# Moving the last block's routing between engines and reordering the first expert tiles in a fused attention and two-mixture kernel

## The chip, the cores and the metric

The kernel runs on one core of a Trainium2 chip. The metric is device time in microseconds (us) from launch to end, taken as the median of several executions; one further execution is profiled, and its trace is what all rows below come from. Engines are named as the profile names them: PE (matmul; PEld is its weight load), DVE (vector), ACT (scalar), POOL (GpSimd) and SP (the queue that issues most DMA transfers). Each engine works through its own instructions strictly in program order and waits on semaphores for the others.

## The reference

Three stages, 1152 rows (tokens) of 512 columns between them. The change lies where the third begins.

```python
x = attention(q, k, v, f)                 # 2 batches x 8 heads x 576 x 64, causal, with decay from f
x = moe(x, domain_probs, w1, w2)          # dense: all 4 experts on every row

def moe2(x, w_skip, w_gate, w1, w2):      # routed: 8 experts, one for each row
    do_compute = x @ w_skip > 0           # the other rows are returned as they are
    xc = x[do_compute]
    logits = xc @ w_gate
    e_idx = argmax(logits, axis=1)
    probs = softmax(logits)
    gate_w = probs[row, e_idx]
    y[e_idx == e] = gate_w * (relu(xc[e_idx == e] @ w1[e]) @ w2[e])
    out[do_compute] = xc + y
```

## The kernel before

Rows are worked in nine blocks of 128 (NB = 9, so L = 8 is the last). The dense mixture ends with its last half expert's down products: `down_block` (36 matmuls a block on PE), then `add_block` on DVE, which leaves the block's final rows in `acc[:, t]`. While PE still works on later blocks, each finished block is routed by a plan written out by hand (`plan`, `planned`): `store` writes it to the output and, for the first five blocks, to a DRAM copy `xda`; `turn` transposes it; `logits` (or the folded form) gives nine columns, eight gate scores and the skip score; `choose` (five small DVE instructions) makes the one-hot mask `mall` of the chosen expert; `prefix` counts with two small matmuls how many earlier rows chose the same expert and puts that rank into `rank`; `slots` turns the rank into a one-hot row of 128 slots (`onehot`); `keep` stores `d` (scores less their maximum) and two token numbers into `perm`; `count` adds the mask to a running sum `macc`; `tokens` multiplies `onehot` by `perm`, which gives for each expert the list of its rows in slot order (`pids`).

Two blocks, 7 and 8, are still to be routed when the last down product is done, and nothing of the dense stage is left to lie beside them. This stretch, from the end of `down_block` for block 8 (line 989 on) to the first expert's up products, I call the turn. The order there is the order of the code: the scheduler is in manual mode, and each engine takes its instructions as written.

The routed stage works with small tiles. For each expert e the first 64 rows in its list are half rows of 256 columns on 128 partitions (two partitions a row), handled by class `Few`: `x_in` transposes them on PE and copies them with ACT into `xt`, `up(0)` and `up(1)` multiply by the up weights (eight matmuls in all, seen as sixteen passes in the trace, since each f32 matmul shows as two), a relu on ACT gives `hs`, `turn` transposes that on PE and copies it in two halves (DVE, then ACT) into `ht`, and `down` multiplies by the down weights (sixteen matmuls, 32 passes), after which DVE adds the gated result to the rows (`xes[e]`) and POOL scatters them to the output. Experts with over 64 rows spill into two further tiles of class `Many`. The rows of experts 1 to 7 come by an indirect DMA issued on POOL (`gather`), from lists that `idx` holds. Expert 0 is not gathered, so that PE has work at once: its rows of blocks 0 to 4 come early from `xda` into `xs0`; its rows of blocks 5 to 8 are picked out of `acc` on chip, by `mine` (the mask's first column as f32), `pick` (a 128x64 one-hot matrix `sel`) and `select` (matmuls of `sel` with `acc`, summed over the blocks in the PSUM bank `xsel`). `xs0` plus `xsel` is then transposed and copied into `xt0`.

Weights of the routed stage come in chunks of 1 MB into a ring of 17 places, in the order of use; `load_m` issues them on SP, and each waits until its place is free. Chunks 0 to 14 are issued before or in the turn. Chunks 15 and 16 go to a pool (`wraw2`) that takes over memory of the routing pools, so they wait for the last routing work that uses it, which is `weigh` (softmax weights for blocks 3 to 8: exponentials on ACT, then DVE). Chunks 17 and 18 take the places of expert 0's up weights, 19 and 20 those of its down weights, 21 and 22 those of expert 1's up weights. `heat` is two matmuls whose result nobody reads.

After the turn, before the change, PE does: up of tile 0; `gates` (nine small matmuls on `perm`, which wait for `weigh`); turn of tile 0; x_in of tile 1; down of tile 0; up(0) of tile 1; x_in of tile 2; up(1) of tile 1; then a loop whose step i does up(0) of tile i+1, turn of tile i, x_in of tile i+2, up(1) of tile i+1, down of tile i. `place` and `spread` on DVE prepare the lists for the two spill tiles.

Of the kernel before, what the change touches and what calls it, by code (L numbers as in the profile page):

```python
# [7 lines left out]
F32 = mybir.dt.float32  # L8
# [39 lines left out]
def kernel(  # L48
# [613 lines left out]
    with ExitStack() as mo:  # L662
# [19 lines left out]
                T.transpose(ps[:, (c - c0) * P:(c - c0 + 1) * P], acc[:, t, c * P:(c + 1) * P], ident)  # L682
            A.copy(out=xt[:, c0 * P:c1 * P], in_=ps[:, 0:(c1 - c0) * P])

        def logits(t, lp):
            xt = rt[t]["xt"]
            rt[t]["lp"] = lp
            for c in range(KD):
                T.matmul(out=lp[:, 0:E2 + 1], lhsT=xt[:, c * P:(c + 1) * P], rhs=wgs[:, c, :],
                         start=(c == 0), stop=(c == KD - 1))  # L690

# [191 lines left out]
        def cleared(t):  # L883
            rows = hida_p.tile([P, 8, HD], F32, tag="hh0", name="rows")
            rowo = hida_p.tile([P, 8, HD], F32, tag="hl0", name="rowo")
            G.memset(rows[:, 1:E2], 0.0)
            G.memset(rowo[:, 0:2 * KO], 0.0)
            xes.extend([xs0] + [rows[:, e] for e in range(1, E2)])
            xos.extend(rowo[:, 2 * k:2 * k + 2].rearrange("p a c -> p (a c)") for k in range(KO))
            ys.extend(rowo[:, 2 * KO + i] for i in range(4))  # L890

# [96 lines left out]
        def heat(n):  # L988
            for _ in range(n):
                T.matmul(out=hot[:, 0:3 * P], lhsT=ones, rhs=onehot[:, 0:3, :], start=True, stop=True)  # L990

        L = NB - 1
        for tb in range(NA - 1, NB):
            ps = down_block(UL, tb, planned)
            if tb < L:
                add_block(UL, tb, ps, 0, DM)
        h = DM // 2
        logits(L - 1, ps_r.tile([P, 512], F32, tag="lg", name=f"lg_{L - 1}"))
        add_block(UL, L, ps, 0, h)
# [5 lines left out]
        store(L)  # L1005
        load_m(13, 15)
        pf = ps_d.tile([P, 512], F32, tag="d", name="pf")
        hot = ps_d.tile([P, 512], F32, tag="d", name="hot")
        xsel = ps_u.tile([P, 512], F32, tag="u", name="xsel")

        def mine(t):
            m32 = rt[t]["m32"] = rtile([P, 1], "m32", t)
            V.tensor_copy(out=m32, in_=mall[:, t, 0:1])

        def pick(t):
            m32 = rt[t]["m32"]
            V.tensor_scalar(out=sel[:, t - NX, :], in0=slotn[:, 0:RT], scalar1=rank[:, t:t + 1],
                            scalar2=m32, op0=ALU.is_equal, op1=ALU.mult)

        def select(t):  # L1020
            for g in range(2):
                T.matmul(out=xsel[RT * g:RT * g + RT, 0:HD], lhsT=sel[:, t - NX, :],
                         rhs=acc[:, t, g * HD:(g + 1) * HD], start=(t == NX), stop=(t == L))

        for t in range(NX, NA):
            mine(t)
            pick(t)
        choose(L - 1)
        mine(L - 1)
        count(L - 1)  # L1030
        select(NX)
        logits(L, ps_u.tile([P, 512], F32, tag="u", name=f"lg_{L}"))
        keep(L - 1)
        prefix(L - 1, pf)
        for t in range(NX + 1, NA):
            select(t)
        heat(2)
        choose(L)
        mine(L)
        pick(L - 1)  # L1040
        pf = ps_u.tile([P, 512], F32, tag="u", name="pf_L")
        prefix(L, pf)
        select(L - 1)
        pick(L)
        select(L)
        slots(L - 1)
        V.tensor_tensor(out=xs0, in0=xsel[:, 0:HD], in1=xs0, op=ALU.add)
        heat(2)
        slots(L)
        keep(L)  # L1050
        count(L)
        xtp0 = ps_r.tile([P, 512], F32, tag="xp", name="xtp0")
        for c in range(2):
            T.transpose(xtp0[:, c * P:(c + 1) * P], xs0[:, c * P:(c + 1) * P], ident)
        A.copy(out=xt0, in_=xtp0[:, 0:HD])
        tokens(L - 1)
        tokens(L)
        V.scalar_tensor_tensor(out=idx, in0=pids[:, 1, :], scalar=2.0, in1=pida, op0=ALU.mult, op1=ALU.add)
        T.matmul(out=pf[:, E2:2 * E2], lhsT=ones, rhs=macc[L], start=True, stop=True)
        V.tensor_copy(out=cnt, in_=pf[:, E2:2 * E2])  # L1060
        weigh(3, NB)

# [55 lines left out]
    class Few:  # L1118
# [12 lines left out]
        def up(self, half):  # L1131
            for c in range(2 * half, 2 * half + 2):
                g, j = divmod(c, 2)
                for h in range(2):
                    T.matmul(out=self.ps[RT * h:RT * h + RT, :], lhsT=self.xt[:, j * P + RT * g:j * P + RT * g + RT],
                             rhs=wm[0, self.e, h][:, c, :], start=(c == 0), stop=(c == KD - 1))
            if half:
                A.activation(out=self.hs[:, 0:HF], in_=self.ps, func=AF.Relu)

        def turn(self):  # L1140
            for j in range(4):
# [132 lines left out]
        listed(po, KO, idxo, gato)  # L1274

    tiles = [Few(e) for e in range(E2)] + [Many(k) for k in range(KO)]
    for e in range(1, E2):
        gather(xes[e], idx[:, e:e + 1])
    load_m(15, NS + 2)
    tiles[0].up(0)  # L1280
    tiles[0].up(1)
    gates()
    tiles[0].turn()
    tiles[1].x_in()
    tiles[0].down()
    place()
    tiles[1].up(0)
    tiles[2].x_in()
    tiles[1].up(1)
    spread(0, NB)  # L1290
    ahead = {(E2 - 3, 1): [(0, 0, 0)], (E2 - 2, 1): [(0, 0, 1)], (E2 - 1, 0): [(1, 0, 0)],
             (E2 - 1, 1): [(1, 0, 1), (0, 1, 0)], (E2, 0): [(0, 1, 1)], (E2, 1): [(1, 1, 0), (1, 1, 1)]}

# [120 lines left out]
```

## Time and profile before

| | us |
|---|---|
| median of 3 executions | 605.55 |
| lowest, highest | 604.0, 605.95 |
| the profiled execution's own time | 604.57 |
| span of its trace, first to last instruction | 602.9 |

| engine | busy us | share of the span |
|---|---|---|
| PE | 588.6 | 98% |
| PEld | 489.5 | 81% |
| POOL | 331.1 | 55% |
| DVE | 321.8 | 53% |
| ACT | 262.2 | 44% |

The profiled execution's time is 1.67 us longer than its span, and 0.98 us under the median. A share is a mean over stages: PE's 98% says that PE is the engine to follow, and only the stretches where it is not at work without a break, or works on what nobody needs, can give time back. The times of rows are us from the span's start.

### The profile page before, as it was taken

The numbers are of one execution on the slowest core, as the hardware profiler recorded it, in microseconds if no ns is written. First come the engines' busy times: TensorE is split into PE (matmuls) and PEld (weight loads), VectorE is DVE, ScalarE is ACT, GpSimd is POOL, SyncE is SP. The second block draws the span as 40 slices with busy tenths as digits, with TensorE's granted clock in tenths as the row PEclk, the third lists the DMA queues.
The fourth block names the chain that finished last, engine by engine and source line by source line (L and its number), as shares of the span: only waits on it lengthen the run. The fifth ranks groups of instructions, "written<-read, shape, count | busy, mean of one in ns | idle before, by whom it ended". The sixth has DMA issues, their size and how long they took to land. (4 is left out here: it accounts for less than half of the span.)

```text
span 602.9 us, 10704 instructions
## 1 busy us (share of the span) xinstructions
PE 588.6 (98%) x3975; PEld 489.5 (81%) x3975; DVE 321.8 (53%) x826; ACT 262.2 (44%) x665; POOL 331.1 (55%) x380
## 2 busy tenths in 40 slices
PE   8999899999999999999999999999999999999995
PEld 5788777998898998998988989989989774555674
DVE  6877877655444544534535535535535466411483
ACT  5678788684243343334324315315314222112481
POOL 4869997799268159249339429519615143222421
PEclk7899999999999999999999999999999999999998
DMA  6786550301111011101202201202255975999940
GB/s 209 229 308 212 186 187 23 132 16 67 70 70 62 10 52 35 55 8 63 71 1 70 72 1 70 71 1 70 71 210 212 369 276 194 416 418 421 401 157 24
DMA packets 19127, 84.22 MB, mean 140 GB/s; under 512 B 2943, under 2 KB 3977, under 8 KB 11905
## 3 DMA queue, kind: packets, MB, share of 16 engines
q1 hardware_dynamic: 16832, 73.19, 33.3%
q0 software_dynamic: 2240, 10.32, 4.4%
q8 instruction: 32, 0.52, 0.4%
q14 instruction: 23, 0.18, 0.1%
HBM read 79.44 MB, written 5.28 MB: 141 GB/s over the span
## 5 line engine op out<-in xcount | busy, mean ns | idle before, releaser
L865 PE MATMUL dn<-w2h,hh 128*128 128x512 f32 x288 | 114.4, 397 | 0.0
L867 PE MATMUL dn<-w2h,hl 128*128 128x512 f32 x288 | 112.5, 391 | 0.0
L866 PE MATMUL dn<-w2l,hh 128*128 128x512 f32 x288 | 112.2, 390 | 0.0
L877 DVE SCALAR_TENSOR_TENSOR acc<-dn,dps,acc 128x512 f32<-128x512 f32 (+1 forms) x64 | 47.4, 742 | 98.3 <-PE dn L867 98.2
L156 POOL TENSOR_TENSOR w2l<-rawd,w2h 128x512 fp32r<-128x512 f32 x32 | 40.5, 1296 | 94.4 <-ACT w2h L201 94.4
L220 PE MATMUL p<-xb_h,w 128*128 128x320 f32 x224 | 69.2, 309 | 0.0
L219 PE MATMUL p<-xb_l,w 128*128 128x320 f32 x224 | 69.2, 309 | 0.0
L218 PE MATMUL p<-xb_h,w 128*128 128x320 f32 x224 | 69.1, 309 | 0.0
L867 PEld LDWEIGHTS dn<-w2h,hl 128*128 128x128 f32 x288 | 54.0, 188 | 11.6
L865 PEld LDWEIGHTS dn<-w2h,hh 128*128 128x128 f32 x288 | 54.1, 188 | 11.2 <-issue 1.4
L866 PEld LDWEIGHTS dn<-w2l,hh 128*128 128x128 f32 x288 | 54.1, 188 | 10.0
L218 PE MATMUL p<-xa,w 128*128 128x256 f32 x218 | 61.3, 281 | 0.0
L220 PE MATMUL p<-xa,w 128*128 128x256 f32 x218 | 61.2, 281 | 0.0
L219 PE MATMUL p<-xa,w 128*128 128x256 f32 x218 | 61.2, 281 | 0.0
L201 ACT CAST w2h<-rawd 128x512 fp32r<-128x512 f32 x32 | 18.3, 622 | 84.7 <-PE dn L867 84.7
L156 POOL TENSOR_TENSOR hl<-m,hh 128x256 fp32r<-128x256 f32 (+1 forms) x32 | 25.9, 810 | 43.5 <-ACT hh L827 43.5
L821 DVE SCALAR_TENSOR_TENSOR hl<-p,hh 128x320 fp32r<-128x320 f32 (+1 forms) x62 | 28.5, 459 | 36.1 <-ACT hh L820 36.1
L156 POOL TENSOR_TENSOR w<-ws,w 128x512 fp32r<-128x512 f32 x32 | 40.7, 1294 | 3.4 <-ACT w L175 3.4
L219 PEld LDWEIGHTS p<-xb_l,w 128*128 128x128 f32 x224 | 42.0, 188 | 0.3
L218 PEld LDWEIGHTS p<-xb_h,w 128*128 128x128 f32 x224 | 42.1, 188 | 0.3
L220 PEld LDWEIGHTS p<-xb_h,w 128*128 128x128 f32 x224 | 42.0, 188 | 0.0
L218 PEld LDWEIGHTS p<-xa,w 128*128 128x128 f32 x218 | 41.3, 190 | 0.3
(292 smaller groups left out, 1329.0 us busy)
## 6 DMA issues: line engine op xcount, KB each, us to landing
wm<-in_m SPq DMA_DIRECT2D x32, 1024.0 KB, 9.7
rawu<-in_w SPq DMA_DIRECT2D x8, 1024.0 KB, 4.7
rawd<-in_w SPq DMA_DIRECT2D x8, 1024.0 KB, 4.7
qk<-in_qk SPq DMA_DIRECT2D x7, 640.0 KB, 5.5
qk<-in_qk SPq DMA_DIRECT2D x7, 576.0 KB, 4.0
bias<-nbd SPq DMA_DIRECT2D x14, 288.0 KB, 6.1
v<-in_v SPq DMA_DIRECT2D x8, 320.0 KB, 3.0
bias<-nbd SPq DMA_DIRECT2D x16, 144.0 KB, 5.9
```

The source lines that it names most:

```text
L156: eng.tensor_tensor(out=out, in0=a, in1=b, op=ALU.subtract)
L201: A.copy(out=ws["d", u][0][:, c, :], in_=wr["d", u][:, c, :])
L218: T.matmul(out=ps, lhsT=wt[:, 0, a, i, :], rhs=xh[:, i, :], start=(i == 0), stop=False)
L219: T.matmul(out=ps, lhsT=wt[:, 0, a, i, :], rhs=xl[:, i, :], start=False, stop=False)
L220: T.matmul(out=ps, lhsT=wt[:, 1, a, i, :], rhs=xh[:, i, :], start=False, stop=(i == 1))
L821: V.scalar_tensor_tensor(out=hl[:, j, cs], in0=c, scalar=0.0, in1=hh[:, j, cs].bitcast(F32), op0=ALU.max, op1=ALU.subtract)
L865: T.matmul(out=ps, lhsT=hh[:, j, ks], rhs=wh[:, j, :], start=(j == 0), stop=False)
L866: T.matmul(out=ps, lhsT=hh[:, j, ks], rhs=wl[:, j, :], start=False, stop=False)
L867: T.matmul(out=ps, lhsT=hl[:, j, ks], rhs=wh[:, j, :], start=False, stop=(j == 3))
L877: V.scalar_tensor_tensor(out=a, in0=ps[:, c0:c1], scalar=pe, in1=a, op0=ALU.mult, op1=ALU.add)
```

## The change

In the turn, `mine`, `pick` for blocks 5 and 6, `count` and the token part of `keep` go from DVE to POOL; `pick` for blocks 7 and 8 stays on DVE. `logits` of block 8 is split in two, with the prefix of block 7 between. Block 8's rows of expert 0 are no longer selected into `xsel`: the sum of blocks 5 to 7 is added to `xs0` earlier, transposed by matmuls with `ident` into a new bank `xtl`, and four more matmuls with `acc` as the weights and `sel` as the moving operand add block 8's rows into the same open bank, already transposed. `xt0` is copied out of it in two halves, by ACT and by DVE. The second `heat` moves behind the count of all rows.

Since `xs0` now lacks block 8's rows, the rows that tile 0's result is added to come by an eighth gather, second in the order (1, 0, 2 to 7); `rows` is cleared whole. In the first body x_in and up(0) of tile 1 stand directly behind tile 0's up products, its turn, `gates` and `spread` behind those, and its down products behind up(1) of tile 1.

```diff
--- before.py
+++ after.py
@@ -682,10 +682,10 @@
                 T.transpose(ps[:, (c - c0) * P:(c - c0 + 1) * P], acc[:, t, c * P:(c + 1) * P], ident)
             A.copy(out=xt[:, c0 * P:c1 * P], in_=ps[:, 0:(c1 - c0) * P])
 
-        def logits(t, lp):
+        def logits(t, lp, c0=0, c1=KD):
             xt = rt[t]["xt"]
             rt[t]["lp"] = lp
-            for c in range(KD):
+            for c in range(c0, c1):
                 T.matmul(out=lp[:, 0:E2 + 1], lhsT=xt[:, c * P:(c + 1) * P], rhs=wgs[:, c, :],
                          start=(c == 0), stop=(c == KD - 1))
 
@@ -883,9 +883,9 @@
         def cleared(t):
             rows = hida_p.tile([P, 8, HD], F32, tag="hh0", name="rows")
             rowo = hida_p.tile([P, 8, HD], F32, tag="hl0", name="rowo")
-            G.memset(rows[:, 1:E2], 0.0)
+            G.memset(rows, 0.0)
             G.memset(rowo[:, 0:2 * KO], 0.0)
-            xes.extend([xs0] + [rows[:, e] for e in range(1, E2)])
+            xes.extend(rows[:, e] for e in range(E2))
             xos.extend(rowo[:, 2 * k:2 * k + 2].rearrange("p a c -> p (a c)") for k in range(KO))
             ys.extend(rowo[:, 2 * KO + i] for i in range(4))
 
@@ -989,11 +989,27 @@
             for _ in range(n):
                 T.matmul(out=hot[:, 0:3 * P], lhsT=ones, rhs=onehot[:, 0:3, :], start=True, stop=True)
 
+        def mine(t, eng=V):
+            m32 = rt[t]["m32"] = rtile([P, 1], "m32", t)
+            eng.tensor_copy(out=m32, in_=mall[:, t, 0:1])
+
+        def pick(t, eng=V):
+            eng.tensor_scalar(out=sel[:, t - NX, :], in0=slotn[:, 0:RT], scalar1=rank[:, t:t + 1],
+                              scalar2=rt[t]["m32"], op0=ALU.is_equal, op1=ALU.mult)
+
+        def select(t):
+            for g in range(2):
+                T.matmul(out=xsel[RT * g:RT * g + RT, 0:HD], lhsT=sel[:, t - NX, :],
+                         rhs=acc[:, t, g * HD:(g + 1) * HD], start=(t == NX), stop=(t == L - 1))
+
         L = NB - 1
         for tb in range(NA - 1, NB):
             ps = down_block(UL, tb, planned)
             if tb < L:
                 add_block(UL, tb, ps, 0, DM)
+        for t in range(NX, NA):
+            mine(t, G)
+            pick(t, G)
         h = DM // 2
         logits(L - 1, ps_r.tile([P, 512], F32, tag="lg", name=f"lg_{L - 1}"))
         add_block(UL, L, ps, 0, h)
@@ -1005,58 +1021,45 @@
         store(L)
         load_m(13, 15)
         pf = ps_d.tile([P, 512], F32, tag="d", name="pf")
-        hot = ps_d.tile([P, 512], F32, tag="d", name="hot")
         xsel = ps_u.tile([P, 512], F32, tag="u", name="xsel")
-
-        def mine(t):
-            m32 = rt[t]["m32"] = rtile([P, 1], "m32", t)
-            V.tensor_copy(out=m32, in_=mall[:, t, 0:1])
-
-        def pick(t):
-            m32 = rt[t]["m32"]
-            V.tensor_scalar(out=sel[:, t - NX, :], in0=slotn[:, 0:RT], scalar1=rank[:, t:t + 1],
-                            scalar2=m32, op0=ALU.is_equal, op1=ALU.mult)
-
-        def select(t):
-            for g in range(2):
-                T.matmul(out=xsel[RT * g:RT * g + RT, 0:HD], lhsT=sel[:, t - NX, :],
-                         rhs=acc[:, t, g * HD:(g + 1) * HD], start=(t == NX), stop=(t == L))
-
-        for t in range(NX, NA):
-            mine(t)
-            pick(t)
         choose(L - 1)
-        mine(L - 1)
-        count(L - 1)
+        mine(L - 1, G)
+        count(L - 1, G)
         select(NX)
-        logits(L, ps_u.tile([P, 512], F32, tag="u", name=f"lg_{L}"))
-        keep(L - 1)
+        lgl = ps_u.tile([P, 512], F32, tag="u", name=f"lg_{L}")
+        logits(L, lgl, 0, 2)
         prefix(L - 1, pf)
-        for t in range(NX + 1, NA):
+        pick(L - 1)
+        logits(L, lgl, 2, 4)
+        for t in range(NX + 1, L):
             select(t)
+        keep(L - 1, G)
+        choose(L)
+        mine(L, G)
+        V.tensor_tensor(out=xs0, in0=xsel[:, 0:HD], in1=xs0, op=ALU.add)
+        hot = ps_r.tile([P, 512], F32, tag="xp", name="hot")
+        xtl = ps_d.tile([P, 512], F32, tag="d", name="xtl")
         heat(2)
-        choose(L)
-        mine(L)
-        pick(L - 1)
         pf = ps_u.tile([P, 512], F32, tag="u", name="pf_L")
         prefix(L, pf)
-        select(L - 1)
         pick(L)
-        select(L)
+        for c in range(2):
+            T.matmul(out=xtl[:, c * P:(c + 1) * P], lhsT=xs0[:, c * P:(c + 1) * P], rhs=ident, start=(c == 0), stop=False)
+        for c in range(KD):
+            g, j = divmod(c, 2)
+            T.matmul(out=xtl[:, j * P + RT * g:j * P + RT * g + RT], lhsT=acc[:, L, c * P:(c + 1) * P],
+                     rhs=sel[:, L - NX, :], start=False, stop=(c == KD - 1))
         slots(L - 1)
-        V.tensor_tensor(out=xs0, in0=xsel[:, 0:HD], in1=xs0, op=ALU.add)
-        heat(2)
         slots(L)
-        keep(L)
-        count(L)
-        xtp0 = ps_r.tile([P, 512], F32, tag="xp", name="xtp0")
-        for c in range(2):
-            T.transpose(xtp0[:, c * P:(c + 1) * P], xs0[:, c * P:(c + 1) * P], ident)
-        A.copy(out=xt0, in_=xtp0[:, 0:HD])
+        A.copy(out=xt0[:, 0:P], in_=xtl[:, 0:P])
+        V.tensor_copy(out=xt0[:, P:HD], in_=xtl[:, P:HD])
+        keep(L, G)
+        count(L, G)
         tokens(L - 1)
         tokens(L)
         V.scalar_tensor_tensor(out=idx, in0=pids[:, 1, :], scalar=2.0, in1=pida, op0=ALU.mult, op1=ALU.add)
         T.matmul(out=pf[:, E2:2 * E2], lhsT=ones, rhs=macc[L], start=True, stop=True)
+        heat(2)
         V.tensor_copy(out=cnt, in_=pf[:, E2:2 * E2])
         weigh(3, NB)
 
@@ -1134,8 +1137,11 @@
                 for h in range(2):
                     T.matmul(out=self.ps[RT * h:RT * h + RT, :], lhsT=self.xt[:, j * P + RT * g:j * P + RT * g + RT],
                              rhs=wm[0, self.e, h][:, c, :], start=(c == 0), stop=(c == KD - 1))
-            if half:
-                A.activation(out=self.hs[:, 0:HF], in_=self.ps, func=AF.Relu)
+            if half and self.e:
+                self.relu()
+
+        def relu(self):
+            A.activation(out=self.hs[:, 0:HF], in_=self.ps, func=AF.Relu)
 
         def turn(self):
             for j in range(4):
@@ -1274,20 +1280,21 @@
         listed(po, KO, idxo, gato)
 
     tiles = [Few(e) for e in range(E2)] + [Many(k) for k in range(KO)]
-    for e in range(1, E2):
+    for e in (1, 0, *range(2, E2)):
         gather(xes[e], idx[:, e:e + 1])
     load_m(15, NS + 2)
     tiles[0].up(0)
     tiles[0].up(1)
-    gates()
-    tiles[0].turn()
     tiles[1].x_in()
-    tiles[0].down()
+    tiles[0].relu()
     place()
     tiles[1].up(0)
+    tiles[0].turn()
+    gates()
+    spread(0, NB)
     tiles[2].x_in()
     tiles[1].up(1)
-    spread(0, NB)
+    tiles[0].down()
     ahead = {(E2 - 3, 1): [(0, 0, 0)], (E2 - 2, 1): [(0, 0, 1)], (E2 - 1, 0): [(1, 0, 0)],
              (E2 - 1, 1): [(1, 0, 1), (0, 1, 0)], (E2, 0): [(0, 1, 1)], (E2, 1): [(1, 1, 0), (1, 1, 1)]}
 
```

On DVE, from the last block's additions to the start of block 8's choice. `m` is what `mine` makes, `lg` the scores, `pr` and `rank` the prefix. Before, five rows stand between the mask of block 7 and its prefix, and four more (`m` and `sel` of blocks 5 and 6) stand ahead of the first row here:

```order
L708 TENSOR_REDUCE mx_6121<-lg_6089 128x1
L710 SCALAR_TENSOR_TENSOR sc_6123<-lg_6089,mx_6121,rev 128x8
L712 TENSOR_REDUCE sm_6125<-sc_6123 128x1
L714 TENSOR_SCALAR msk_6127<-lg_6089 128x1
L716 SCALAR_TENSOR_TENSOR mall<-sc_6123,sm_6125,msk_6127 128x8
L1013 CAST m_7_6130<-mall 128x1
L744 TENSOR_TENSOR macc_6132<-macc_6084,mall 128x8
L723 TENSOR_SCALAR d_6141<-lg_6089,mx_6121 128x8
L724 TENSOR_SCALAR perm<-mall,tokp 128x8
L725 TENSOR_SCALAR perm<-mall 128x8
L733 ISA pr_6147,rank<-pf,mall 128x8
```

The same place on DVE now:

```order
L712 TENSOR_REDUCE sm_6124<-sc_6122 128x1
L714 TENSOR_SCALAR msk_6126<-lg_6095 128x1
L716 SCALAR_TENSOR_TENSOR mall<-sc_6122,sm_6124,msk_6126 128x8
L733 ISA pr_6140,rank<-pf,mall 128x8
L733 ISA rank 128x1
L997 TENSOR_SCALAR sel<-slotn,rank,m_7_6129 128x64
L723 TENSOR_SCALAR d_6149<-lg_6095,mx_6120 128x8
L708 TENSOR_REDUCE mx_6153<-lg_6135 128x1
```

The prefix now follows the mask directly, and block 7's `pick` (`sel`) has moved ahead of block 8's choice, where it stood behind it.

On PE, the end of the turn, as the difference; `pf_L` is block 8's prefix, `xtp` the old transposed bank, `xtl` the new one:

```order
-L1022 MATMUL xsel<-acc,sel 64x256 x4
-L990 LDWEIGHTS ones
-L990 MATMUL hot<-onehot,ones 128x384
-L990 LDWEIGHTS ones
-L990 MATMUL hot<-onehot,ones 128x384
-L1054 MATMUL xtp_6186<-ident,xs_2078 128x128 x2
+L731 MATMUL pf_L<-macc_6131,ones 128x8
+L1047 MATMUL xtl<-ident,xs_2078 128x128 x2
+L1050 MATMUL xtl<-sel,acc 128x64 x4
```

Block 8's selection, with its way through DVE and back, is replaced by four products behind the transposes.

On PE, the first body now, from tile 0's last up products (`up` with weights `wm` of chunk 1) to its turn (`tp<-ident,hs`); `tpx<-ident,rows` is x_in of tile 1:

```order
L1138 MATMUL up_6263<-wm_5387,xt_2079 64x512
L1131 MATMUL tpx<-ident,rows 128x128 x2
L1138 MATMUL up_6264<-wm_5617,xt_6241 64x512
L1138 MATMUL up_6264<-wm_5627,xt_6241 64x512
L1138 MATMUL up_6264<-wm_5617,xt_6241 64x512
L1138 MATMUL up_6264<-wm_5627,xt_6241 64x512
L1148 MATMUL tp<-ident,hs_6246 128x128 x4
```

Up(0) of tile 1 needs the copy of what the instruction just ahead of it makes; before, turn of tile 0 and down of tile 0 stood around x_in.

## Rows read from the trace of the kernel before

Timeline rows give start, duration, engine, line, operation, output from inputs, shapes and a count; in brackets stands the idle time just before and what ended it. In the first group the columns are the stretch, its length, then PE, PEld, DVE, ACT and POOL busy time (instructions), granted PE clock, DMA share and GB/s.

**Rows 1.** Busy time by stretch: around the turn, and the expert bodies.

```profile
500.00:510.00 10.00, 9.39 (x62) 4.09 (x61) 7.58 (x47) 2.24 (x16) 2.96 (x3) 1.00 0.74 263
520.00:596.00 76.00, 75.76 (x492) 46.67 (x489) 30.95 (x45) 28.13 (x45) 20.58 (x19) 1.00 0.79 320
```

**Rows 2.** Timeline of DVE in the turn.

```profile
499.04 0.88 DVE L877 SCALAR_TENSOR_TENSOR acc<-dn,dps,acc 128x256 f32<-128x256 f32 x2 [0.28 <-PE dn L867]
...
500.65 0.16 DVE L708 TENSOR_REDUCE mx<-lg 128x1 f32<-128x8 f32 x1
...
502.22 0.16 DVE L708 TENSOR_REDUCE mx<-lg 128x1 f32<-128x8 f32 x1
...
502.94 0.23 DVE L716 SCALAR_TENSOR_TENSOR mall<-sc,sm,msk 128x8 bf16<-128x8 f32 x1
...
503.70 0.31 DVE L1017 TENSOR_SCALAR sel<-slotn,rank,m 128x64 f32<-128x64 f32 x1
...
504.76 0.42 DVE L1047 TENSOR_TENSOR xs<-xsel,xs 128x256 f32<-128x256 f32 x1 [0.56 <-PE xsel L1022]
...
505.98 0.17 DVE L1058 SCALAR_TENSOR_TENSOR idx<-pids,pida 128x8 int32<-128x8 f32 x1 [0.19 <-PE pids L750]
```

**Rows 3.** Timeline of PE and ACT in the turn.

```profile
498.84 0.95 PE L689 MATMUL lg<-wgs,xt 128*128 128x9 f32 x8
...
500.47 0.38 ACT L683 COPY xt<-xpb 128x256 f32<-128x256 f32 x1
...
500.96 1.06 PE L689 MATMUL lg<-wgs,xt 128*128 128x9 f32 x8
...
504.65 0.50 PE L990 MATMUL hot<-onehot,ones 128*128 128x384 bf16 x2
...
505.25 0.44 PE L1054 MATMUL xtp<-ident,xs 128*128 128x128 f32 x2
...
505.72 0.37 ACT L1055 COPY xt<-xtp 128x256 f32<-128x256 f32 x1 [4.87 <-PE pids L750]
...
506.15 3.65 PE L1135 MATMUL up<-wm,xt 128*64 128x512 f32 x16
```

**Rows 4.** Timeline of PE in the first bodies.

```profile
510.19 0.30 PE L1228 MATMUL yp<-perm,onehot 128*128 128x24 bf16 x6 [0.22 <-DVE perm L770]
...
511.76 3.67 PE L1150 MATMUL yp<-wm,ht 128*64 128x256 f32 x32 [0.30 <-DVE ht L1143]
...
517.08 0.44 PE L1128 MATMUL tpx<-ident,rows 128*128 128x128 f32 x2
517.45 2.79 PE L1135 MATMUL up<-wm,xt 128*64 128x512 f32 x12
```

**Rows 5.** Gathers one and two, then three and four: durations in ns, starts, landing.

```profile
L640 POOL DMA_INDIRECT rows<-out,idx x2: 998/1046/1094, 506.4 to 507.8; - x2
...
DMA to landing us min/median/max: 3.0/3.0/3.0
...
L640 POOL DMA_INDIRECT rows<-out,idx x2: 998/1008/1019, 509.1 to 510.5; - x2
...
DMA to landing us min/median/max: 2.6/4.4/6.2
```

**Rows 6.** SP's queue: the first weight chunks behind the turn.

```profile
510.34 2.05 SPq L147 DMA_DIRECT2D wm<-in_m  x4
```

**Rows 7.** DVE's slots instruction alone, then beside POOL's clearing of the rows.

```profile
486.36 0.29 DVE L737 TENSOR_SCALAR onehot<-slotn,rank 128x128 bf16<-128x128 f32 x1
...
489.95 1.55 DVE L737 TENSOR_SCALAR onehot<-slotn,rank 128x128 bf16<-128x128 f32 x1
...
490.47 0.95 POOL L887 MEMSET rowo<- 128x1024 f32 x1
```

**Rows 8.** Chunk 29, issued at 535.2 us: time to landing, and its first use.

```profile
DMA to landing us min/median/max: 26.2/26.2/26.2
...
563.53 3.62 PE L1150 MATMUL yp<-wm,ht 128*64 128x256 f32 x32
```

## Prediction

> **What bounds the kernel now.** I read the busy time by stretch first. From 520 to 596 us PE is at work for 75.76 of 76.00 us at granted clock 1.00, so the expert bodies are a PE stream without a break: whatever moves their start moves the end by as much, unless weights then come late. From 500 to 510 PE is busy 9.39 us and DVE 7.58 [rows 1]; DVE's sum is no full load, but its timeline shows one serial chain, and PE's busy time there holds two pairs of heat matmuls that no one reads. So the turn is a latency chain, DVE to PE and back, and the question is what ends last on it.
>
> The chain, read forwards. Block 8's second addition ends at 499.92 (499.04 + 0.88); block 7's choice starts at 500.65, though its scores were done at 499.79 (498.84 + 0.95): DVE was held by the four small instructions of blocks 5 and 6. Block 8's choice starts at 502.22, its mask ends at 503.17 (502.94 + 0.23), block 8's pick ends at 504.01, the sum of picked rows at 505.18, idx starts at 505.98 [rows 2, 3]. The transposes start at 505.25, the copy into xt0 runs 505.72 to 506.09, up of tile 0 starts at 506.15 [rows 3].
>
> **The change, part by part, against the profiled execution (604.57 us, 0.98 under the median).**
>
> *Work leaves DVE ahead of block 7's choice.* It can start at about 499.9 in place of 500.65, 0.75 us earlier. That is not passed on whole. Block 8's choice needs its scores, whose second half needs the copy that ends at 500.85 (500.47 + 0.38) and then half of a group of eight passes that took 1.06, so 0.5, with the prefix of block 7 and the tail of a pass around it: about 501.9 [rows 3]. DVE meanwhile has the rank, the pick and d of block 7 to do and is free at about 502.0. I take 502.0: 0.2 us earlier than 502.22 [rows 2]. The bound moves from DVE to both engines at once, which is why 0.75 becomes 0.2.
>
> *From block 8's mask to up of tile 0: 506.15 - 503.17 = 2.98 us before.* Now: the addition of 0.42 stands ahead of the rank where a pick of 0.31 stood, so block 8's pick ends 0.84 + 0.1 = 0.94 after the mask (504.01 - 503.17 = 0.84) [rows 2]. Then four f32 products with 128-column weights: eight passes, 0.95 by the group of eight at 498.84 [rows 3]. Then two half copies. No row shows a copy of 128 columns here; it lies between nothing and the 0.37 of 256 columns [rows 3], and I take 0.28. They write one tile, and a half waits for the other: where ht is copied so, down of tile 0 waited 0.30 for it [rows 4]. So 0.56, plus some 0.2 for four handovers of about 0.05 (506.15 - 506.09 = 0.06 is one) [rows 3]. Together 0.94 + 0.95 + 0.56 + 0.2 = 2.65, 0.3 less than before. PE's tokens, the count and the moved heat (at most 0.50 [rows 3]) lie beside the copies; with slower copies they cost nothing, with faster ones heat ends last, so at most some 0.2. Up of tile 0 starts about 0.5 us earlier, near 505.65.
>
> *POOL's share.* Blocks 5 and 6 are long done with when their picks are needed, so these cost nothing. Blocks 7 and 8 make POOL work while DVE picks. The nearest row on what that costs DVE is the slots instruction, 0.29 us alone and 1.55 us beside POOL's clearing, ending at 491.50, just after POOL's 491.42 (490.47 + 0.95) [rows 7]: 1.26 us for a POOL run far longer than these. Below, nothing: POOL's instructions may fall between. Above, two picks on the chain, each held by less than the 0.31 that a pick itself takes [rows 2], 0.6 in all. The instructions are short, so I take 0.1. The Trainium skill, page "SBUF — State Buffer", section "Who interferes with whom", says that DVE in a two-port mode and GpSimd lock each other out for a whole instruction, the second to issue waiting. The trace agrees in the 1.55 us [rows 7]; by that rule every overlap would be paid, and the sum would take the upper bound. The larger clearing of rows (2048 columns for 1792) lies beside down products; no wait follows from it but at most its own seventh part, about 0.2, on one slots instruction, which I count in the range.
>
> *The first body.* Its PE work is the same. Two waits go: 0.22 for the softmax weights and 0.30 for ht [rows 4]. One comes: up(0) of tile 1 now follows its own x_in directly. Transposes to dependent product took 506.15 - 505.25 = 0.90 in the turn [rows 3]; x_in to the next product, where nothing depends, took 517.45 - 517.08 = 0.37 [rows 4]. So 0.53 is added, 0.52 removed: nothing. Behind PE's wait at x_in stands the whole stream, so this price is real. place, spread, relu and the turn copies have 1.8 us of PE work and more as cover, and the result of tile 0 is not wanted soon.
>
> *Gathers.* idx follows the second half copy on DVE; it moves from 505.98 to about 505.7. Gather one landed 3.0 us after its issue at 506.4 [rows 5], now at about 509.1; PE needs it after up of tile 0, at 505.65 + 3.65 = 509.3: hidden by 0.2. The extra gather goes second, so tile 2's is third, 2.7 us after the first (509.1 - 506.4): about 508.85. It is needed at about 513.0 (509.2, 0.9 for x_in, 1.8 for half of up, 0.5 each for turn and gates). Its landing is the uncertain part. Gather three before, issued 1.2 us ahead of the first weight chunk at 510.34, took 2.6; gather four, 0.1 us behind it, took 6.2 [rows 5, 6]. The weights move up too: the exponentials start behind ACT's copy, which now ends 0.8 earlier, less some waiting for d, so the chunks come at about 509.65, 0.8 us behind the gather. On a line between 2.6 and 6.2 that is 3.7 us, landing at 512.6: hidden by 0.4. At 6.2 it lands at 515.05, and PE stands for 2.05.
>
> *Weights.* Chunks 15 to 18 come 0.7 us earlier. Chunks 19 and 20 wait for tile 0's down, now about 3 us later, but four chunks ahead of them keep the transfers busy. The closest of the chunks that I followed is 29: landing at 561.4 (535.2 + 26.2), used at 563.53, 2.1 us of slack [rows 8]. It moves with the stream.
>
> Sum: up of tile 0 earlier by 0.5, POOL beside DVE 0.1 back, body 0. The profiled execution would take 604.57 - 0.4 = 604.2, and the median 605.55 - 0.4, **605.1 us**.
>
> **The rivals.**
>
> *Gather three behind the weights (slower).* Place: x_in of tile 2. Mechanism: the chunks start earlier, the gather later, and its 128 rows share the transfer engines with 1 MB chunks. It decides as soon as it takes over 4.1 us (513.0 - 508.85). Full price 2.05, net 1.65 slower: 607.2 on the median. For: 6.2 in the row. Against: the lead of 0.8. The Trainium skill, page "DMA: Bandwidth & Descriptors", section "Queues, rings and completion order", says each engine takes turns between queues packet by packet, by which a gather is slowed but not queued behind whole chunks; the 6.2 shows the slowing.
>
> *DVE locked by POOL (little or nothing gained).* Every overlap is paid, 0.6 for the 0.1 taken: up of tile 0 moves by -0.1 to +0.1, and the median is 605.6. This is the lock rule's own result. Against: POOL's instructions are few and short.
>
> *DVE's saving passed on whole (faster).* If PE's scores come early enough, block 8's choice starts at about 500.9 (499.9 + 0.95 for a choice + 0.06), 1.3 us earlier, not 0.2; with the 0.3 behind and both body waits gone, about 1.8: 603.7. Against: the copy ending at 500.85, ahead of which no second half of scores can start [rows 3].
>
> *The clock.* The change moves heat and lets PE wait at another place. At 1.2 in place of 2.4 GHz up of tile 0 would double, 3.65 more [rows 3]: 608.8. Against: the granted clock is 1.00 throughout a turn with less PE work [rows 1].
>
> **How the numbers follow.** Forecast 0.62; gather three late 0.15; lock 0.12; whole saving 0.07; clock 0.04. Medians of so few executions scatter by up to 1 us around their middle (604.0 to 605.95). The range takes in the lock and most of the late gather, and downwards the forecast's bounds (0.2 more from the copies, none lost to POOL) with the scatter: 603.9 to 606.9. About 0.3%, 1.8 us, is what a measurement of this kernel can tell from no change. Faster by more needs the whole saving or a lucky scatter: 0.09. Slower by more needs the clock, or the late gather at full price with the scatter: 0.10. Within: 0.81.
>
> **What would show it.** Right: block 8's choice near 502.0, up of tile 0 near 505.65, a wait of about half a microsecond ahead of up(0) of tile 1, none ahead of x_in of tile 2, and the bodies behind it an unbroken stream. Wrong: picks on DVE over 0.31 us, x_in of tile 1 or 2 waiting for a transfer, a clock under 1.00 between 500 and 515, or a wait of PE for weights after 520.

## The result: the time after, and where it went

The changed kernel took 612.28 us in the median of five executions (612.13 to 613.9), beside 605.32 for the kernel before in the same session (604.0 to 605.95). The ratio is 1.0118, with a 95% interval of 1.0097 to 1.0138: 7 us slower, where 0.4 less was forecast and 606.9 was the upper end of the range. The profiled execution took 612.13 with a span of 610.3.

The loss is in one place. This is busy time by stretch of the kernel after; columns are us, then busy us of each engine with its instructions, the granted clock, and the share and rate of the DMA engines:

```profile
500.00:505.00 5.00, 4.91 (x41) 3.30 (x41) 3.60 (x21) 0.65 (x2) 1.66 (x8) 1.00 0.79 270
505.00:510.00 5.00, 4.77 (x30) 1.80 (x28) 3.13 (x19) 1.42 (x13) 0.72 (x1) 1.00 0.51 208
510.00:515.00 5.00, 0.02 (x2) 0.00 (x0) 1.92 (x13) 0.00 (x0) 3.78 (x5) 0.87 0.82 300
515.00:520.00 5.00, 4.20 (x10) 1.05 (x10) 0.00 (x0) 0.87 (x2) 3.63 (x4) 0.50 1.02 407
520.00:525.00 5.00, 5.00 (x43) 3.03 (x43) 3.19 (x13) 1.24 (x3) 0.00 (x0) 0.94 0.67 260
```

PE does next to nothing from 510 to 515, and works at clock 0.50 (1.2 GHz) from 515 to 520. Its timeline names the wait (start, us, operation, and in brackets the idle time before it with what ended it):

```profile
506.36 3.65 PE L1138 MATMUL up<-wm,xt 128*64 128x512 f32 x16 [0.23 <-DVE xt L1055]
515.34 0.66 PE L1131 MATMUL tpx<-ident,rows 128*128 128x128 f32 x2 [5.32 <-DMA rows<-out,idx]
516.46 3.68 PE L1138 MATMUL up<-wm,xt 128*64 128x512 f32 x8 [0.46 <-ACT xt L1132]
520.07 0.88 PE L1148 MATMUL tp<-ident,hs 128*128 128x128 f32 x4
...
523.12 3.62 PE L1156 MATMUL yp<-wm,ht 128*64 128x256 f32 x32
526.58 1.89 PE L1138 MATMUL up<-wm,xt 128*64 128x512 f32 x8
```

The first rows of tile 1, gather one, come 5.32 us after PE is ready for them, and the half of up behind them takes 3.68 where the same eight products took 1.89 to 1.94 at full clock. From up of tile 0 to up(0) of tile 2 it is 20.22 us (526.58 - 506.36), before 13.07 (519.22 - 506.15). That start in the kernel before is read from the weight load of the first product:

```profile
519.22 0.14 PEld L1135 LDWEIGHTS up<-wm,xt 128*64 128x64 f32 x2 [0.28 <-issue]
```

Behind that, PE runs on without waits (74.76 us busy from 525 to 600).

Gather one is late twice over. DVE wrote its list, idx, at 506.36; then, on POOL:

```profile
504.27 0.20 POOL L744 TENSOR_TENSOR macc<-macc,mall 128x8 bf16<-128x8 bf16 x1
509.28 1.15 POOL L640 DMA_INDIRECT rows<-out,idx  x1 [4.81 <-DVE perm L770]
510.73 1.00 POOL L640 DMA_INDIRECT rows<-out,idx  x1 [0.30 <-issue]
```

The list was done at 506.52 (506.36 + 0.16) and POOL had nothing else to do, yet it issued the gather 2.76 us later; before, the same step took 0.28. Coming out only 0.5 ahead of the first weight chunk (509.80), the gather then took 5.9 to land, and 3.0 before [rows 5]:

```profile
DMA to landing us min/median/max: 5.9/5.9/5.9
```

The releaser in brackets, DVE's perm, is a guess of the page's: by the program, gather one waits for idx and for the stores of out, and the last of these had landed by 502.5 (issued 500.3, 2.2 to landing). What held POOL from 506.52 to 509.28 was the question of the experiments.

### The profile page after: what moved, and what is told of

It reads as the page before. It is cut to its first block, busy times and chain, and to the rows that moved or that the text cites. A ratio compares the mean times of both kernels' runs of the same rounds, so it can differ in the third digit from the quotient of the medians.

```text
span 610.3 us, 10726 instructions
## 1 busy us (share of the span) xinstructions
PE 590.8 (97%) x3981; PEld 490.8 (80%) x3981; DVE 319.9 (52%) x815; ACT 262.1 (43%) x665; POOL 337.0 (55%) x393
```

## The theories

**T1, the next page of instructions.** The DMA list of the trace has a queue of kind "instruction". A packet does not say which engine it is for. Of those of 8192 bytes, three come, in the kernels before and after alike, when POOL has 65, 193 and 323 instructions recorded, so about every 128, and are taken to be POOL's. The next one came at 508.83 before, with 452 recorded, in the middle of the gathers. After, the change puts 15 more instructions on POOL ahead of gather one, whose first instruction becomes the 461st recorded of POOL where it was the 446th; the packet comes at 507.36, with 460 recorded. So POOL would have run out of instructions just ahead of the gather. The stretch 507.3 to 507.7 of the kernel after (queue and kind: packets, MB, share):

```profile
q1 hardware_dynamic: 21, 0.07, 45.1%
q14 instruction: 1, 0.01, 4.8%
```

**T2, DVE in POOL's way.** DVE's chain of gate weights ran from 507.17 to past 509.2, just as long as POOL stood, and could keep it from writing the gather's descriptors. **T3, the weights.** Chunks 13 and 14, issued at 500.7 and under way until about 508, could hold the gather itself.

## Experiments on the stall

**e1 and e2: the same kernel, POOL's stream shifted.** In folds(), which runs at 429 us:

```diff
+            for _ in range(24):        # e2: 128
+                G.memset(zero, 0.0)
             G.memset(wgz, 0.0)
```

The 24 clearings of e1 stand some 75 us ahead of the gather, behind other work of POOL:

```profile
429.17 3.71 POOL L912 MEMSET zero<- 128x1 f32 x24
```

The expectations put them at 410 us and POOL idle there, which the trace does not bear out. The 128 of e2 take 20 us, and the last block's additions begin at the same time in both (499.67 and 499.62), so this makes no difference between them.

> The changed kernel with 24 more one-element clearings on POOL at about 410 us, where POOL is idle; nothing else differs. In the changed kernel POOL issued gather one at 509.28, 2.76 us after its list of rows was done (506.52), against 0.28 in the kernel before. Theory T1 (POOL ran out of fetched instructions: the trace shows an 8 KB packet of the instruction queue at 507.36, and the gather is the instruction of POOL's stream that follows it): 24 more instructions ahead of it move that gap to an earlier place of the stream, where POOL waits for others anyway, so gather one starts about 0.3 after its list, lands near 510 to 512, and the time is 604.5 to 606. Rival T2 (DVE's chain of weights at 507.2 to 509.2 keeps POOL from writing the gather's descriptors): the chain is unchanged, so gather one again starts at the chain's end, 2.5 to 2.8 after its list, and the time stays at 611.5 to 613. Rival T3 (the weight chunks in flight at 504 to 508 hold the gather itself): also no change, 611.5 to 613.

> The changed kernel with 128 such clearings in place of 24: 128 instructions are one 8 KB packet of the instruction queue by the counts between packets in the trace (64 bytes each), so the gap falls on the same instruction of POOL's stream as in the changed kernel without them. T1: gather one is late again by 2 to 3 us after its list, time 611 to 613.5. T2 and T3: late too, 611.5 to 613. If the clearings as such helped or hurt, this run would show it: a time of 604.5 to 606 here would speak against T1's reading of e1.

e1 took 606.5 us beside 606.05 for the kernel before on that chip, ratio 1.0004 (0.9986 to 1.0022); that is 0.5 above what was expected, and a second wait was left, told below. e2 took 611.19, ratio 1.0081 (1.0049 to 1.0113). In e1 the packet came at 492.50, there was none between 503.5 and 508, and POOL went straight to gather one, 0.29 after its list (506.84):

```profile
504.60 0.20 POOL L744 TENSOR_TENSOR macc<-macc,mall 128x8 bf16<-128x8 bf16 x1
507.13 1.12 POOL L640 DMA_INDIRECT rows<-out,idx  x1 [2.33 <-DVE cnt L1065]
```

DVE's chain and the weights were where they had been, so T2 and T3 fall. With 128 clearings, one packet's worth, the stall was back: packet at 507.87 with 588 instructions recorded (460 + 128), gather at 509.81. The clearings as such bring nothing: 128 are slow where 24 are not.

**e4: the kernel before, 15 clearings.** Same edit with range(15), in the kernel before: gather one is the 461st instruction there too.

> The kernel before with 15 more one-element clearings on POOL at about 410 us, which puts gather one at the place of POOL's stream that it has in the changed kernel. T1 if only the place counts: gather one starts 2 to 3 us after its list (0.28 before), x_in of the second tile waits for it, and the time is 608 to 612. T1 if the packet must also be asked for late, under the weights' traffic: the packet comes some us earlier than the gather needs it, and the time stays at 604.5 to 606. T2 and T3: the kernel before as it was, 604.5 to 606. A slow result here would show that the place in the stream alone does it, without any of the change.

606.97 us, ratio 1.0012 (0.9997 to 1.0028), gather one 0.28 after its list: the place in the stream alone costs nothing. Here POOL went on to the gather's waits early, since it had no picks and lists to make in the turn; the packet came at 496.71, with no weights in flight.

**e3 and e7: the weights away.** Both were to keep chunks 13 and 14 out of 501 to 508. e3 moved their issue in the text to the call that issues 15 and on:

> The changed kernel with weight chunks 13 and 14 issued after the turn, together with 15 and those that follow, so that no weights are in flight at 504 to 508; the two chunks come first in that later group. T1 with a refill held up by the weights: the instruction packet is served at about 504 to 505 rather than 507.36, and gather one starts 0.3 to 1 after its list; the time is 604.5 to 607 (the chunks themselves move 2 MB later, for which chunk 29 had 2.1 us of slack in the kernel before). T3 expects the same of the gather, but without a change in the time of the instruction packet. T2: the chain of weights on DVE is unchanged, gather one starts at its end, 2.5 to 2.8 after its list, and the time is 611.5 to 614.

612.47 us, ratio 1.0103 (1.0079 to 1.0127): a failed edit. SP goes through its own queue, and there the two still stood next behind the last store, at 501.50; e3 is the changed kernel once more. e7 gave them to ACT:

```diff
-        load_m(13, 15)
...
-    load_m(15, NS + 2)
...
     tiles[0].relu()
+    load_m(13, 15, A)
+    load_m(15, NS + 2)
     place()
```

> The changed kernel, without added clearings, in which weight chunks 13 and 14 are issued by ACT after tile 0's relu (about 511), so that no weights are in flight at 501 to 508. (In e3 the two issues were moved in the text alone: they were still the next in SP's queue after the last store and went out at the same place, 501.5.) Theory W (POOL asked for its next page of instructions at 503.7 to 504.3, and the page was served only when the weights in flight had ended: 507.36 against 507.6 in the changed kernel, 508.31 against 508.4 in e3, 507.87 against 508.1 in e2): here the page comes at 504 to 505, gather one starts about 0.3 after its list, and the stall of 5.3 at tile 1's rows falls to at most 1; the time is 605 to 608, since the two chunks land some 10 us later. Theory R (the page is asked for only when POOL gets past its wait for the list, and always costs 2 to 2.7 there): the page comes 0.8 to 1 after the list as before, gather one 2.5 to 2.8 after it, and the time stays at 610.5 to 613.

No weights moved (busy us and DMA share of two stretches of e7), and the packet was there at 505.14, in the stretch 505 to 505.5:

```profile
503.00:504.00 1.00, 1.00 (x11) 0.41 (x8) 0.90 (x6) 0.00 (x0) 0.06 (x1) 1.00 0.00 0
504.00:505.00 1.00, 0.91 (x8) 0.67 (x7) 0.85 (x6) 0.00 (x0) 0.76 (x4) 1.00 0.00 0
```

```profile
q14 instruction: 1, 0.01, 3.8%
```

Gather one started 0.28 after its list, at 507.09, and tile 1's rows were in time. The time was 610.69 beside 608.24 on that chip, ratio 1.0044 (1.0023 to 1.0065), above the 605 to 608 expected. In the profiled execution (608.77) the next rows were late instead, and the clock was 0.69 in 515 to 520:

```profile
515.93 0.44 PE L1130 MATMUL tpx<-ident,rows 128*128 128x128 f32 x2 [2.05 <-DMA rows<-out,idx]
```

So the weights matter after all, not to the gather but to the page. The profiled executions together (us; the place is gather one's in POOL's program):

| kernel | place | packet at | list done | gather one issued | delay |
|---|---|---|---|---|---|
| before | 446 | 508.83 | 506.15 | 506.43 | 0.28 |
| after | 461 | 507.36 | 506.52 | 509.28 | 2.76 |
| e1, 24 more | 485 | 492.50 | 506.84 | 507.13 | 0.29 |
| e2, 128 more | 589 | 507.87 | 507.93 | 509.81 | 1.88 |
| e3 | 461 | 508.31 | 507.34 | 510.28 | 2.94 |
| e4, before with 15 more | 461 | 496.71 | 507.90 | 508.18 | 0.28 |
| e7, no weights in flight | 461 | 505.14 | 506.81 | 507.09 | 0.28 |
| e8, heat (below) | 461 | 508.60 | 507.91 | 510.54 | 2.63 |
| e12, after again | 461 | 507.54 | 506.68 | 509.46 | 2.78 |

In the five rows with a stall the gather follows the packet's start by 1.92 to 1.97 us. The packet does not follow the list (0.84 behind it in the kernel after, 0.06 ahead of it in e2). It comes in the last microsecond of the weights' traffic where they are in flight (their last packet ends 0.6 to 1.0 us after its start), and 2.2 us sooner in e7, where none are (2.5 when counted from the start of POOL's last instruction, at 504.27 and 504.56). That the request went out at the same place in e7 and in the kernel after is inferred: the trace shows the packet, not the request. Nor does the traffic hold back every packet of the queue: in the kernel after another one started at 501.83, under way with the weights, and was done 1.53 us later, in the stretch 501.8 to 503.4:

```profile
q1 hardware_dynamic: 72, 0.45, 100.6%
q14 instruction: 1, 0.01, 6.0%
```

So e7 shows that without the weights the page is there in time; why beside them it came only near their end stays open. The Trainium skill, page "Runtime: NRT & Kernel Launch", section "Instruction fetch mechanics", says that an engine fetches its next block by its own DMA queue while it executes and that the cost of crossing into it is mostly hidden. It is hidden in e1, e4, e7 and the kernel before, and delays gather one by 1.88 to 2.94 us in the other rows, so here the measurement decides.

**e9: POOL's new instructions back on DVE.** The masks of blocks 5 to 8, the picks of blocks 5 and 6, and the lists and counts of blocks 7 and 8 lose their argument G, so gather one is the 446th again.

> The changed kernel with one part undone: block 7's and 8's masks, first pick, lists and counts on DVE again, as in the kernel before, 15 fewer instructions on POOL ahead of gather one, no added clearings. Theory (POOL's own new instructions moved the place at which it asks for its next page from the middle of the gathers to the middle of the turn, under the weights): gather one is again the 446th instruction of POOL's stream, it starts 0.28 after its list, and the page comes later, among the gathers; tile 1's rows are there in time. DVE carries some 15 small instructions of 0.15 to 0.35 more, a few of them ahead of the list; the list some 0.3 to 0.8 later than in the changed kernel. Time 605 to 607.5. Rival (the stall belongs to gather one's surroundings, not to the place in the stream): 610.5 to 613.

608.95 beside 605.22, ratio 1.0053 (1.0037 to 1.0069), against 1.012 for e12 on the same chip. The stall was gone (delay 0.28, packet at 510.70 among the gathers), but the time was above what was expected: the turn took 0.97 longer (7.98 for 7.01, at clock 1.00), and a second wait came out, told next.

## Experiments on what lies behind the stall

**e8: heat while PE waits.** Thirty products of ones into an idle bank ahead of tile 1's x_in.

> The changed kernel with 30 products of ones that write an unused bank, put on PE between tile 0's up products and the transposes of tile 1's rows, where PE stood 5.3 us; some 0.16 us each by the heats of the turn, 4.8 together, so they end just before the rows land. What is computed is the same. It prices the clock apart from the wait: in the changed kernel the granted clock was 0.50 in 515 to 520, and the half up products of tile 1 took 3.68 against 1.94 in e1. Theory: the clock stays at 1.00, up takes 1.9, and the time is 610.0 to 611, about 2 less than the 612.3 without them. Rival (the clock is lowered for another reason, or the work that it stretched is hidden behind later waits): 611.8 to 613.

611.15 beside 608.24, ratio 1.0059 (1.0032 to 1.0086). PE's rows of e8, by stretch and on the timeline:

```profile
515.00:520.00 5.00, 3.55 (x19) 1.30 (x17) 0.00 (x0) 0.87 (x2) 3.78 (x5) 1.00 1.01 409
```

```profile
518.25 1.94 PE L1138 MATMUL up<-wm,xt 128*64 128x512 f32 x8 [1.37 <-issue]
```

The clock stayed at 1.00 and the half of up took 1.94 for 3.68. From up of tile 0 to up(0) of tile 2 it is 18.66 us (507.75 to 526.41) for 20.22, so 1.6 of the 7 come back. That is net of a wait ahead of up(0) of tile 1, 1.37 here for 0.46 in the kernel after, which no run takes apart; the rows that the lower clock stretched make 2.2 (below). By the ratios it is 3.6, give or take some 2; the trace is the narrower measure.

**e5, e10, e11: tile 2's rows earlier.** In e1 PE stood 1.28 ahead of tile 2's x_in, in e7 2.05, in e9:

```profile
517.05 0.44 PE L1131 MATMUL tpx<-ident,rows 128*128 128x128 f32 x2 [1.87 <-DMA rows<-out,idx]
```

That gather, the third, was issued at 510.8 in e9 and took

```profile
DMA to landing us min/median/max: 6.2/6.2/6.2
```

The edit, on e1 (e5, and e11 again) and on e9 (e10):

```diff
-    for e in (1, 0, *range(2, E2)):
+    for e in (1, 2, 0, *range(3, E2)):
```

> The kernel of e1 (24 clearings ahead on POOL) with one thing more: the gathers are issued for tiles 1, 2, 0, 3 and on, in place of 1, 0, 2, 3. In e1 PE still stood 1.28 us at 515.38 ahead of the transposes of tile 2's rows, whose gather was the third, issued at 509.85, 0.36 ahead of the first weight chunks (510.21). Theory A (that stall is the third gather's landing behind the weights, the rival of the prediction with 607.2): issued at 508.55, the rows of tile 2 land before 514, the 1.28 goes, and the time is 604.4 to 605.6 against 606.5 for e1. Theory B (PE stood for something else, as the gates' products or a copy): no change against e1, 606 to 607. Tile 0's own rows, now third, are wanted only after its down products at 521, where they have 5 us to spare in e1.

> The kernel of e9 with the gathers for tiles 1, 2, 0, 3 and on. If tile 2's rows are the next wait as in e1 (1.28) and e7 (2.05), this takes 1 to 1.5 off e9: 604 to 606. If e9 had no such wait: no change against e9.

> The kernel of e5 again, beside the others of this call. e5 stood at 0.9962 of the kernel before (0.9947 to 0.9978), on a chip on which the kernel before took 608.24 where it took 605.3 to 606.05 on two others. If the gain is the kernel's: 0.995 to 0.999 again. If it came from the slower runs of the kernel before alone: 0.999 to 1.001, within what can be told from no change.

The wait was gone each time: in e10 tile 2's gather landed in 2.8, and the time fell from 608.95 to 607.24, ratio 1.0026 (1.0013 to 1.0039): the step of 1.7 was near what was expected, and the level above it as e9's was. e5 took 605.5 beside 608.24, ratio 0.9962 (0.9947 to 0.9978), on the chip where the kernel before scattered from 605.73 to 610.82; e11 took 604.88 beside 605.22, ratio 0.9993 (0.9984 to 1.0002). So e5's gain did not repeat, and the best version is level with the kernel before. PE in e11:

```profile
508.68 3.65 PE L1140 MATMUL up<-wm,xt 128*64 128x512 f32 x16 [0.23 <-DVE xt L1057]
512.27 0.44 PE L1133 MATMUL tpx<-ident,rows 128*128 128x128 f32 x2
513.17 1.94 PE L1140 MATMUL up<-wm,xt 128*64 128x512 f32 x8 [0.46 <-ACT xt L1134]
...
521.33 1.89 PE L1140 MATMUL up<-wm,xt 128*64 128x512 f32 x8
```

12.65 us from up of tile 0 to up(0) of tile 2 (521.33 - 508.68), 0.42 less than before.

**e6: the first body's old order, on e1.** gates, turn, x_in of tile 1 and down of tile 0 first, as in the kernel before.

> The kernel of e1 with the first body's order of the kernel before (gates, turn, rows of tile 1, down of tile 0, then up of tile 1) and all else of the change kept. Theory A (the body's new order asks for tile 2's rows some 2.5 us earlier than the old one and so makes the 1.28 wait): the wait goes, the old waits of 0.22 and 0.30 come back, and the time is 604.7 to 606 with what the turn itself saved (0.1 to 0.5 of my steps a and b) left. Theory B (the new order gained what it was meant to and the stall is hidden anyway): 606.5 to 607.2, slower than e1.

607.3 beside 608.24, ratio 0.9993 (0.9981 to 1.0006): 1.8 slower than e5 beside it, and level with e1 by the ratios (1.0004). It lost the wait at tile 2's rows, and PE stood 1.41 ahead of down of tile 0 for the copy of ht, where that was 0.30 in [rows 4]. Why the copy came so late is open; no run takes it apart.

**e12: the changed kernel beside e9 to e11.**

> The changed kernel itself beside e9 to e11, so that the parts stand against it on one chip: 611.5 to 613 where the kernel before takes 605 to 606, a ratio of 1.010 to 1.013.

612.5 beside 605.22, ratio 1.0120 (1.0106 to 1.0135), with PE's wait 5.40 and clock 0.50 in 515 to 520. The result repeats.

## Why the prediction was wrong, step by step

**The step that failed is the one on the gathers:** "Gather one landed 3.0 us after its issue at 506.4 [rows 5], now at about 509.1; [...] hidden by 0.2". It took the issue to follow the list by the 0.28 of the kernel before. The list came at 506.52 and the issue 2.76 later, and then, beside the weights, the landing took 5.9. The prediction had counted what the new instructions on POOL cost DVE, and not that they move every later instruction of POOL's stream, and with it, as inferred above, the moment at which the next page is asked for. With a cover of 0.2 nothing absorbed it: of the 7.57 us between e11 and the kernel after (20.22 - 12.65), 7.50 are the wait of 5.32, 1.74 on the half of up (3.68 - 1.94), and 0.22 on each of the two groups of transposes beside it (0.66 - 0.44, 0.88 - 0.66).

**The turn.** Block 7's choice started at 500.14, ahead of 500.65 as forecast, and block 8's 3.23 us after its block's additions began (502.58 - 499.35), 3.18 before (502.22 - 499.04): not 0.2 earlier. The sum had DVE free at 502.0, but DVE stood 0.84 for block 7's prefix, which PE reaches only behind a selection and the first half of block 8's scores (501.70). Kernel after, DVE, then PE and ACT:

```profile
501.93 0.17 DVE L733 CUSTOM_DVE_ANT_0 pr<-pf,mall 128x8 f32<-128x8 f32 x1 [0.84 <-PE pf L731]
...
502.21 0.32 DVE L997 TENSOR_SCALAR sel<-slotn,rank,m 128x64 f32<-128x64 f32 x1
...
502.58 0.16 DVE L708 TENSOR_REDUCE mx<-lg 128x1 f32<-128x8 f32 x1
...
503.29 0.23 DVE L716 SCALAR_TENSOR_TENSOR mall<-sc,sm,msk 128x8 bf16<-128x8 f32 x1
...
504.18 0.35 DVE L997 TENSOR_SCALAR sel<-slotn,rank,m 128x64 f32<-128x64 f32 x1
...
506.02 0.29 DVE L1055 COPY xt<-xtl 128x128 f32<-128x128 f32 x1 [1.10 <-ACT xt L1054]
```

```profile
504.58 1.10 PE L1050 MATMUL xtl<-sel,acc 128*128 128x64 f32 x8
```

```profile
505.72 0.27 ACT L1054 COPY xt<-xtl 128x128 f32<-128x128 f32 x1 [4.56 <-PE pids L750]
```

From mask to up it is 506.36 - 503.52 = 2.84, forecast 2.65, before 2.98. The pick ends 1.01 after the mask (0.94 forecast), the last products take 1.10 (0.95), and the two half copies, one behind the other as forecast, 0.59 (0.56). Additions to up is 7.01 us (506.36 - 499.35), before 7.11: the turn gained 0.1 where the sum had 0.4.

**POOL beside DVE.** Only the second of the two picks had POOL at work beside it; ahead of the first, POOL was done at 502.00 (501.76 + 0.24):

```profile
501.76 0.24 POOL L725 TENSOR_SCALAR perm<-mall 128x8 bf16<-128x8 bf16 x1
...
504.08 0.23 POOL L725 TENSOR_SCALAR perm<-mall 128x8 bf16<-128x8 bf16 x1
```

The second took 0.35 (504.18 to 504.53), for 0.31 in [rows 2], and the first 0.32: the overlap cost some 0.04 where 0.1 was taken. The locked rival, at up to 0.31 for each pick, falls. The rule that the prediction cites, from the Trainium skill, page "SBUF — State Buffer", section "Who interferes with whom", is not borne out by this one overlap; whether the pick ran in a two-port mode, no run shows.

**The body.** Forecast net nothing, with 0.53 ahead of up(0) of tile 1; that wait was 0.46, and the whole 0.42 shorter (e11). Most of the rest is the gates: from their start to the turn behind them it was 0.85 before (510.58 - 509.73), with the wait of 0.22 in it, and 0.23 in e11 (515.76 - 515.53, to the transposes behind them). So the new order was worth more than forecast, and the term was mis-sized to the safe side; it shows only where rows are in time.

**The rivals.** Gather three behind the weights was right in mechanism and size: full price 2.05 forecast, 1.28, 2.05 and 1.87 seen in e1, e7 and e9, removed by the order of the gathers in e5 and e10. What made the forecast prefer 3.7 us for its landing was a lead of 0.8 ahead of the weights; in e1 the lead was 0.36 (510.21 - 509.85). In the kernel after it is hidden by the larger stall. The clock rival had the right price for a lowered clock and the wrong place: behind PE's wait, not in up of tile 0.

**The sum without the stall** is -0.1 from the turn and -0.4 from the body, close to the -0.4 forecast, but from other terms: the turn gave less and the body more. e11's 604.88 against 605.22 agrees, within what can be told from no change; it needs the reordered gathers too, since e1, without the stall alone, took 606.5 beside 606.05.

## What to carry to other kernels

Before moving small instructions onto an engine whose stream ends in a wait that something urgent hangs on, count where in that stream the instruction packets fall, and what transfers are in flight when the next one is due: a shift by a few instructions can be worth more than the move. Take an unexplained idle time with nothing missing by the program as a reason to look at the instruction queue in the DMA list, and test it by adding idle instructions far ahead. And a transfer hidden by 0.2 us is not hidden.

## What the runs showed of the hardware

- The instruction packets taken for POOL's are 8 KB, about 128 instructions apart. Served late, one held POOL until 1.92 to 1.97 us after its start (five runs); beside 1 MB weight chunks it came within the last microsecond of their traffic, 2.2 us later than without them.
- A gather of 128 rows took 2.6 to 3.0 us to land when issued about 1.2 us or more ahead of the first weight chunk, and 5.6 to 8.7 when issued 0.5 ahead of it or later.
- In the profiled executions of e2, e10 and e11 the granted clock fell in the turn itself. In e11 (500 to 505, 505 to 510):

```profile
500.00:505.00 5.00, 5.00 (x39) 3.44 (x37) 3.25 (x17) 0.65 (x2) 1.65 (x8) 0.85 0.55 177
505.00:510.00 5.00, 4.77 (x31) 2.90 (x31) 2.31 (x13) 1.42 (x13) 1.53 (x5) 0.81 0.73 300
```

Eight products on xsel took 1.95 there for 1.08, and additions to up 8.16 (508.68 - 500.52) for 7.01. That is 1.15 of the 1.9 by which this execution (606.77) lies above e11's median.
